# Linear layer after attention: operand splits packed into three steps, conversion steps moved between block products

## Chip, cores and metric

The kernel runs on one core of a Trainium2 chip. The metric is the device time of one execution in microseconds. Five engines work side by side, each through its own list of instructions in order: PE (TensorE, matrix products), DVE (VectorE), ACT (ScalarE), POOL (GpSimd) and SP (SyncE, which here only issues DMAs).

## What is computed

The reference, cut to what matters. Attention with head mixing gives x, and a two-layer network with silu follows:

```python
scores = einsum('bhij,hg->bgij', scale * matmul(q, k^T), w_pre)
attn = einsum('bhij,hg->bgij', softmax(scores), w_post)
x = matmul(attn, v) as (1792, 768)
h = x @ w_in            # (768, 2048)
g = h * sigmoid(h)
return g @ w_out        # (2048, 768)
```

The two weight matrices come as 64-bit floats; all else is 32-bit.

## The kernel before, in words

**Attention** runs first, in groups, until about 440 us of the profiled execution. The change does not touch it.

**The first linear layer** is a 2x2 block product done with seven block products instead of eight. The code counts them as m = 0 to 6. Each block product has its own weight block (a sum of quarter blocks of `w_in`) and its own activations (`xs`, sums and differences of the attention output). It is done in two runs, u = 0 and 1 (the two halves of the tokens), of HF = 8 steps each. A step is one output tile of 128x448: nine matmuls at line 645, for HC = 3 chunks of the contraction. Each chunk takes three, since both operands are split into a high and a low part: high weights by high activations, high by low, and low by high, in this order. So PE needs the low activations from the fourth matmul of a step on and the low weights from the seventh on. There are 7 x 2 x 8 = 112 steps; step s belongs to block product s // 16. The first two steps are done inside attention. "Block 5" below means the block product m = 5, which is steps 80 to 95.

What one step puts on the queues stands in the last loop of the function (lines 886 to 931), in this order: the product; `ready_part` (split of a piece of weights: ACT copies the high part at line 615, POOL subtracts at 616); `load_part` (a DMA on SP, line 610); `evacuate` of the step before (out of one of seven PSUM banks, by ACT or DVE, with silu on ACT at 816); a delayed sum (836); then the jobs of the list `active`, one stage of each; then the conversion steps.

**Operand splits.** `halve` (line 647) makes the high activations by a copy on ACT (650) and, one step later, the low ones by a subtraction on DVE (652). Run (m, u) reads `ops[u]`, which the run before last used, so its three splits are put on the eight steps of the run right ahead of it, by `put_at` at line 672. `put_at(s, n, todo)` spreads the jobs evenly over n steps. `subtract` (654 to 656) forms the differences of activations on DVE, also by `put_at`.

**Weight pieces.** Each block's weights come in six pieces of four chunks, first to sixth. They are loaded and split over the second run of the block before and the first steps of their own block.

**Conversion.** `convert` (lines 38 to 100) is a generator that turns the 64-bit weights into the 32-bit sums that the block products read. It does 96 conversions, two to a piece of the result: the first half of them, for `w_in`, is done in attention, the rest, for `w_out`, later. A conversion is three steps of the generator, with four instructions on DVE (lines 86, 63, 92, 93), one on ACT (90), one multiplication on POOL (66) and, at every second conversion, four additions on POOL (69 to 72); SP loads its source (47) and stores a finished sum (57). In attention some 60 of the 96 are begun. In the linear layer the table `PACE` says how many steps of the generator a block product takes, spread evenly over its 16 steps. At the first step of the second run of block 6 whatever is left is done at once.

Nothing reorders any of this: the order in the code is the order on each engine.

Of the kernel before, what the change touches and what calls it, by code (L numbers as in the profile page):

```python
# [103 lines left out]
def talking_heads_then_silu_mlp(  # L104
# [46 lines left out]
    HF, HC = NFC // 2, NCC // 2  # L151
# [323 lines left out]
    for n in range(1, len(seq)):  # L475
        p0, p1 = first[n - 1], first[n]
        spread = (0, 0, 0, 0, 2, 2) if n == 1 else (-6, -5, -4, -2, -1, 0) if p1 - p0 == 12 else (-6, -5, -4, -3, -2, -1)
        for h in range(0 if n > 1 else 2 * NE, H, 2):
            i = p0 + spread[h // 2]
# [99 lines left out]
    step_of = {x: s for s, x in enumerate(steps)}  # L579
# [67 lines left out]
    def halve(src, dst):  # L647

        hi, lo = (dst[:, 0], dst[:, 1]) if not isinstance(dst, tuple) else dst
        nc.scalar.copy(out=hi, in_=src)  # L650
        yield
        nc.vector.tensor_sub(out=lo, in0=src, in1=raw(hi))  # L652
# [9 lines left out]
    def put_at(s, n, todo):  # L662

        for m, what in enumerate(todo):
            begin[s + m * n // len(todo)].append(what)
# [3 lines left out]
    for m in range(7):  # L669
        for u in range(NU):  # L670
            if m or u:
                put_at(step_of["i", m, u, 0] - HF, HF - 1, [
                    lambda c=c, u=u, at=SOURCE[m]: halve(xs[u][(*at, c)], ops[u][c]) for c in range(HC)])
    for d, (x, y, z) in enumerate(DIFFER):
        for u in range(NU):
# [204 lines left out]
            queue.dma_start(out=out[row:row + end - n, i * W2:(i + 1) * W2], in_=t[n - c * 128:end - c * 128])  # L880
            n = end

    PACE = (18, 14, 26, 6, 18, 22, 16)
    active, sums_at = [], {}
    prev, accs = None, {}
    for s, (kind, m, u, a) in enumerate(steps):
# [41 lines left out]
        if kind == "i":  # L928
            n = u * HF + a
            for _ in range((n + 1) * PACE[m] // (NU * HF) - n * PACE[m] // (NU * HF)):  # L930
                next(conv, None)
# [27 lines left out]
```

## Time and profile before

| what | value |
| --- | --- |
| median of three runs | 856.02 us (854.14 to 858.73) |
| the profiled execution | 856.93 us, its span 855.2 us, mean clock of PE 0.982 of full speed |
| PE matmul busy | 812.8 us, 95% of the span |
| PE weight load busy | 664.4 us, 78% |
| DVE busy | 625.5 us, 73% |
| ACT busy | 509.1 us, 60% |
| POOL busy | 427.0 us, 50% |
| first linear layer | from about 440.4 to 645.1 us of the span |

Busy times of different engines overlap, so they do not add up to the span. A share over the whole span says little on a stage: the views by stretch below are to be read for that.

### The profile page before, as it was taken

How to read it: one execution, taken by the hardware profiler on the slowest of the kernel's cores; microseconds unless marked ns; L12 is line 12 of the kernel's file. 1: busy time of each engine (PE TensorE's matmuls, PEld its weight loads, DVE VectorE, ACT ScalarE, POOL GpSimd, SP SyncE). 2: the span in 40 equal slices, each digit the busy share in tenths (PEclk: the TensorE clock that was granted, in tenths of full speed). 3: DMA queues.
4: the chain of work that ended last, by engine and by line, in shares of the span. 5: the costliest groups of instructions: out<-in, count | busy, mean ns of one | idle time of the engine just before them, and what ended most of it. 6: DMA issues, size and time to landing. Idle time of an engine off the chain costs nothing.

```text
span 855.2 us, 27554 instructions
## 1 busy us (share of the span) xinstructions
PE 812.8 (95%) x11148; PEld 664.4 (78%) x11148; DVE 625.5 (73%) x1137; ACT 509.1 (60%) x1114; POOL 427.0 (50%) x693
## 2 busy tenths in 40 slices
PE   7989999899989999799899999999999999999997
PEld 5456665566756666566589999998989999999997
DVE  5554776477766777475778799999998888786343
ACT  4675887588877878587756554314576533433330
POOL 6131545444554645363787578457643444433440
PEclk9899999899999999899999999999999999999999
DMA  8668878777797787775545347335522123111133
GB/s 175 182 178 194 214 203 242 209 219 202 208 236 222 207 230 206 203 227 162 167 130 178 118 144 211 92 101 153 176 71 66 47 75 92 55 56 56 56 121 130
DMA packets 156838, 132.90 MB, mean 155 GB/s; under 512 B 52163, under 2 KB 150447, under 8 KB 156711
## 3 DMA queue, kind: packets, MB, share of 16 engines
q1 hardware_dynamic: 153459, 128.11, 52.8%
q10 hardware_dynamic: 2836, 2.37, 1.0%
q8 instruction: 88, 1.44, 0.7%
q0 software_dynamic: 416, 0.66, 0.3%
q14 instruction: 39, 0.32, 0.1%
HBM read 64.01 MB, written 27.53 MB: 107 GB/s over the span
## 4 chain that ended last, share of the span: by engine, by line
PE 71%; DVE 11%; DMA 6%; ACT 5%; issue 3%; POOL 2%; SPq 1%; ACTq 1%; DVEq 0%; POOLq 0%
PE ph L629 12%; PE ph L645 10%; PE pt L629 9%; PE pa L437 9%; PE po L368 8%; PE pt L645 7%; PE pp L399 7%; PE pqk L339 7%; DMA g<-st 4%; DVE nm L405 1%; DVE op L652 1%; ACT e L409 1%; DVE g L836 1%; ACT at L446 1%; DVE cg L92 1%
## 5 line engine op out<-in xcount | busy, mean ns | idle before, releaser
L616 POOL TENSOR_TENSOR wl<-wl,wh 128x384 fp32r<-128x384 f32 (+1 forms) x98 | 143.5, 1480 | 125.1 <-ACT wh L615 118.9
L425 POOL TENSOR_SCALAR wr<-wpost,r 128x60 f32<-128x60 f32 x184 | 72.1, 405 | 181.1 <-DVE r L422 125.0
L405 DVE TENSOR_REDUCE nm<-pp 128x1 f32<-128x448 f32 x184 | 105.9, 617 | 71.5 <-PE pp L399 70.9
L409 ACT ACTIVATE e<-pp,nm 128x448 f32<-128x448 f32 x184 | 115.4, 631 | 41.9 <-DVE nm L405 39.3
L437 PEld LDWEIGHTS pa<-wr,e 64*64 64x64 f32 (+1 forms) x5888 | 98.0, 132 | 47.1 <-issue 28.1
L437 PE MATMUL pa<-wr,e 64*64 64x60 f32 (+1 forms) x5888 | 110.4, 221 | 15.9 <-ACT at L446 7.7
L66 POOL TENSOR_TENSOR cg<-cw,cg 128x256 f32<-128x256 f32 x96 | 75.6, 787 | 72.3 <-DVE cw L63 71.4
L399 PE MATMUL pp<-g,wpre 64*64 64x448 f32 x736 | 100.8, 570 | 4.8 <-ACT e L409 4.8
L446 ACT COPY at<-pa 120x960 f32<-120x960 f32 x92 | 90.0, 978 | 5.3 <-PE pa L437 5.3
L368 PE MATMUL po<-at,v 120*64 120x120 f32 (+1 forms) x1536 | 89.6, 271 | 3.3 <-issue 3.3
L368 PEld LDWEIGHTS po<-at,v 120*64 120x64 f32 x1536 | 78.7, 141 | 15.4 <-issue 7.2
L645 PE MATMUL ph<-op,wh 128*128 128x448 f32 x384 | 88.9, 367 | 0.5 <-DVE op L652 0.5
L344 DVE COPY st<-pqk 120x448 f32<-120x448 f32 (+1 forms) x89 | 54.7, 617 | 36.4 <-PE pqk L339 22.2
L645 PEld LDWEIGHTS ph<-op,wh 128*128 128x128 f32 x384 | 71.9, 188 | 7.0 <-DVE op L652 0.9
L90 ACT ACTIVATE cg<-cg,ebias 128x256 int32<-128x256 int32 x96 | 49.6, 517 | 42.0 <-DVE cg L86 40.7
L615 ACT CAST wh<-wl 128x384 fp32r<-128x384 f32 (+1 forms) x98 | 52.0, 554 | 33.3 <-DMA wl<-wi_dram 26.2
L92 DVE SCALAR_TENSOR_TENSOR cg<-cw,cg 128x256 int32<-128x256 int32 x96 | 56.3, 586 | 18.6 <-ACT cg L90 18.3
L645 PE MATMUL pt<-op,wh 128*128 128x448 f32 x288 | 66.7, 366 | 0.6 <-ACT op L650 0.5
L645 PEld LDWEIGHTS pt<-op,wh 128*128 128x128 f32 x288 | 54.0, 188 | 5.6 <-ACT op L650 0.9
L339 PEld LDWEIGHTS pqk<-kh,qh 64*120 64x120 f32 (+1 forms) x186 | 19.0, 177 | 46.9 <-issue 17.9
L346 ACT COPY st<-pqk 120x448 f32<-120x448 f32 (+1 forms) x89 | 48.0, 539 | 6.2 <-PE pqk L339 4.6
L339 PE MATMUL pqk<-kh,qh 64*120 64x448 f32 (+1 forms) x186 | 47.2, 467 | 4.5 <-issue 2.2
(154 smaller groups left out, 1746.2 us busy)
## 6 DMA issues: line engine op xcount, KB each, us to landing
g<-st SPq DMA_DIRECT2D x132, 210.0 KB
cw<-in_moe_w_in SPq DMA_DIRECT2D x48, 256.0 KB
cw<-in_moe_w_out SPq DMA_DIRECT2D x48, 256.0 KB
wi_dram<-cg SPq DMA_DIRECT2D x24, 448.0 KB
wo_dram<-cg SPq DMA_DIRECT2D x24, 448.0 KB
wl<-wi_dram SPq DMA_DIRECT2D x42, 256.0 KB
wl<-wo_dram SPq DMA_DIRECT2D x56, 192.0 KB
g<-st SPq DMA_DIRECT2D x48, 175.0 KB
```

The costliest lines, as they stand in the source:

```text
L66: nc.gpsimd.tensor_mul(out=e, in0=m, in1=e)
L339: nc.tensor.matmul(ps[i][:m, :S], lhsT=q_[rows, hh, :m], rhs=k_[rows], start=(step == 0), stop=(step == 2))
L368: nc.tensor.matmul(po[i * D:(i + 1) * D, c * m:(c + 1) * m], lhsT=vs[b, h][:, i, j, :], rhs=ats[n][:, j, h + i, :m], start=(j == 0), stop= ...
L399: nc.tensor.matmul((self, other)[r].p[HP * c:HP * (c + 1), :S], lhsT=wpre[rows], rhs=gs[self.n][rows, o // R + c * np + p, :], start=True, ...
L405: nc.vector.tensor_reduce(out=self.nm, in_=self.p[:GP, :S], axis=AX.X, op=ALU.max, negate=True)
L409: nc.scalar.activation(out=self.e, in_=self.p[:GP, :S], func=AF.Exp, bias=self.nm, scale=1.0, accum_out=sums)
L425: nc.gpsimd.tensor_scalar(out=g.wr, in0=wpost.rearrange("p g i -> p (g i)"), scalar1=r[:, i:i + 1], scalar2=1.0, op0=ALU.mult, op1=ALU.mult)
L437: nc.tensor.matmul(half[64 * c:64 * c + m, s, j * GH:(j + 1) * GH], lhsT=g.e[rows, j * JT + c * JH:j * JT + c * JH + m], rhs=g.wr[rows], s ...
L446: nc.scalar.copy(out=ats[self.n].rearrange("p j g t -> p (j g) t")[:, :, o:o + 2 * R].rearrange("p x (c i) -> p x c i", i=RH), in_=pa[:KV] ...
L616: nc.gpsimd.tensor_sub(out=wl, in0=raw(wl), in1=raw(wh))
L629: nc.tensor.matmul(p[:, :W2], lhsT=x, rhs=w, start=(g == 0 and n == 0), stop=(g == FG - 1 and n == len(todo) - 1))
L645: nc.tensor.matmul(p[:, :T], lhsT=w, rhs=x, start=(n == 0), stop=(n == len(todo) - 1))
```

## The change

The three splits of a run are put on the first three steps of the run ahead of it, where they stood on its steps 0, 2 and 4; and ten steps of the generator are moved from blocks 5 and 6 to blocks 0 and 1. The sum of `PACE` stays 120.

```diff
     for m in range(7):
         for u in range(NU):
             if m or u:
-                put_at(step_of["i", m, u, 0] - HF, HF - 1, [
+                put_at(step_of["i", m, u, 0] - HF, HC, [
                     lambda c=c, u=u, at=SOURCE[m]: halve(xs[u][(*at, c)], ops[u][c]) for c in range(HC)])
...
-    PACE = (18, 14, 26, 6, 18, 22, 16)
+    PACE = (22, 20, 26, 6, 18, 18, 10)
```

No instruction is added or taken away on any engine, and PE's list is the same. What moves shows on the other engines. First DVE, in the steps ahead of block 5 (tiles `op00` to `op02` are the three low operands of its first run, L838 takes a product out of PSUM, L836 is a delayed sum, L86, L63, L92 and L93 are conversion). Before, ending at the third low operand:

```order
L838 TENSOR_TENSOR g111_8865<-g111_8865,ph_10163 128x448
L836 TENSOR_TENSOR g016_8854<-g016_8854,g116_8870 128x448
L86 TENSOR_SCALAR cg_10141<-cw_10055 128x256
L63 SCALAR_TENSOR_TENSOR cw_9996<-cw_9996 128x256
L838 TENSOR_TENSOR g112_8866<-g112_8866,pt_10178 128x448
L836 TENSOR_TENSOR g017_8855<-g017_8855,g117_8871 128x448
L652 TENSOR_TENSOR op01_8365<-x101_125,op01_8365 128x448
L838 TENSOR_TENSOR g113_8867<-g113_8867,pt_10199 128x448
L92 SCALAR_TENSOR_TENSOR cg_10141<-cw_10055,cg_10141 128x256
L93 TENSOR_SCALAR cw_10055<-cw_10055 128x256
L838 TENSOR_TENSOR g114_8868<-g114_8868,pt_10215 128x448
L652 TENSOR_TENSOR op02_8366<-x102_126,op02_8366 128x448
```

The same place after the change, from the first low operand to the third:

```order
L652 TENSOR_TENSOR op00_8364<-x100_124,op00_8364 128x448
L86 TENSOR_SCALAR cg_10212<-cw_10075 128x256
L63 SCALAR_TENSOR_TENSOR cw_9996<-cw_9996 128x256
L838 TENSOR_TENSOR g111_8865<-g111_8865,ph_10196 128x448
L836 TENSOR_TENSOR g016_8854<-g016_8854,g116_8870 128x448
L652 TENSOR_TENSOR op01_8365<-x101_125,op01_8365 128x448
L838 TENSOR_TENSOR g112_8866<-g112_8866,pt_10220 128x448
L836 TENSOR_TENSOR g017_8855<-g017_8855,g117_8871 128x448
L652 TENSOR_TENSOR op02_8366<-x102_126,op02_8366 128x448
```

The third subtraction (`op02`) now follows the second after one evacuation and one sum; before, two evacuations and half a conversion stood between, and two more evacuations stood ahead of it altogether. The conversion here is a later one, by about three.

Next POOL, at the pieces of weights for block 6 (each L616 is one piece; these are its first to fourth). Before:

```order
L616 TENSOR_TENSOR wl_10490<-wl_10490,wh_10533 128x512
L616 TENSOR_TENSOR wl_10517<-wl_10517,wh_10553 128x512
L66 TENSOR_TENSOR cg_10499<-cw_10388,cg_10499 128x256
L616 TENSOR_TENSOR wl_10536<-wl_10536,wh_10574 128x512
L66 TENSOR_TENSOR cg_10499<-cw_10422,cg_10499 128x256
L69 TENSOR_TENSOR cg_10499<-cg_10499 128x128
L70 TENSOR_TENSOR cg_10499<-cg_10499 128x128
L71 TENSOR_TENSOR cg_10499<-cg_10499 128x128
L72 TENSOR_TENSOR cg_10499<-cg_10499 128x128
L616 TENSOR_TENSOR wl_10577<-wl_10577,wh_10616 128x512
```

After:

```order
L616 TENSOR_TENSOR wl_10521<-wl_10521,wh_10555 128x512
L66 TENSOR_TENSOR cg_10503<-cw_10369,cg_10503 128x256
L616 TENSOR_TENSOR wl_10538<-wl_10538,wh_10576 128x512
L616 TENSOR_TENSOR wl_10558<-wl_10558,wh_10592 128x512
L66 TENSOR_TENSOR cg_10503<-cw_10420,cg_10503 128x256
L69 TENSOR_TENSOR cg_10503<-cg_10503 128x128
L70 TENSOR_TENSOR cg_10503<-cg_10503 128x128
L71 TENSOR_TENSOR cg_10503<-cg_10503 128x128
L72 TENSOR_TENSOR cg_10503<-cg_10503 128x128
L616 TENSOR_TENSOR wl_10595<-wl_10595,wh_10632 128x512
```

In both, a multiplication and four additions stand ahead of the fourth piece. Before they belong to conversion 93 (counted from 0) and two more conversions are still behind; after they belong to conversion 95, the last.

Last POOL at the pieces for block 3, again the first to the fourth. Before:

```order
L616 TENSOR_TENSOR wl_9629<-wl_9629,wh_9671 128x512
L66 TENSOR_TENSOR cg_9636<-cw_9529,cg_9636 128x256
L616 TENSOR_TENSOR wl_9654<-wl_9654,wh_9696 128x512
L616 TENSOR_TENSOR wl_9674<-wl_9674,wh_9713 128x512
L66 TENSOR_TENSOR cg_9636<-cw_9561,cg_9636 128x256
L69 TENSOR_TENSOR cg_9636<-cg_9636 128x128
L70 TENSOR_TENSOR cg_9636<-cg_9636 128x128
L71 TENSOR_TENSOR cg_9636<-cg_9636 128x128
L72 TENSOR_TENSOR cg_9636<-cg_9636 128x128
L66 TENSOR_TENSOR cg_9721<-cw_9598,cg_9721 128x256
L616 TENSOR_TENSOR wl_9716<-wl_9716,wh_9761 128x512
```

After:

```order
L616 TENSOR_TENSOR wl_9671<-wl_9671,wh_9714 128x512
L616 TENSOR_TENSOR wl_9688<-wl_9688,wh_9734 128x512
L66 TENSOR_TENSOR cg_9696<-cw_9596,cg_9696 128x256
L616 TENSOR_TENSOR wl_9717<-wl_9717,wh_9754 128x512
L66 TENSOR_TENSOR cg_9696<-cw_9616,cg_9696 128x256
L69 TENSOR_TENSOR cg_9696<-cg_9696 128x128
L70 TENSOR_TENSOR cg_9696<-cg_9696 128x128
L71 TENSOR_TENSOR cg_9696<-cg_9696 128x128
L72 TENSOR_TENSOR cg_9696<-cg_9696 128x128
L616 TENSOR_TENSOR wl_9757<-wl_9757,wh_9797 128x512
```

Before, the four additions stand one multiplication ahead of the fourth piece, and that multiplication (L66) is the last thing it stands behind; after, the last multiplication has its four additions behind it, and the fourth piece comes after them.

## Rows read from the trace of the kernel before

**Rows 1.** The head of the page: span.

```profile
span 855.2 us, 27554 instructions
```

**Rows 2.** Windows by block product 0 to 6; each engine: busy us (x instructions), granted clock.

```profile
440.40:466.04 25.64, 25.64 (x128) 23.78 (x127) 21.62 (x40) 15.91 (x35) 16.91 (x21) 1.00 0.46 144
466.04:495.23 29.19, 29.19 (x146) 27.05 (x144) 24.18 (x41) 16.86 (x31) 17.25 (x22) 1.00 0.44 139
495.23:524.41 29.18, 29.18 (x145) 27.05 (x144) 28.17 (x45) 17.18 (x36) 24.08 (x29) 1.00 0.56 175
524.41:553.59 29.18, 29.18 (x145) 27.05 (x144) 27.11 (x43) 9.47 (x19) 18.35 (x19) 1.00 0.35 102
553.59:582.79 29.20, 29.20 (x145) 26.97 (x144) 28.92 (x50) 8.18 (x16) 17.36 (x18) 1.00 0.51 154
582.79:613.61 30.82, 29.92 (x146) 26.88 (x144) 28.92 (x55) 15.69 (x31) 21.50 (x29) 1.00 0.48 149
613.61:645.08 31.47, 29.98 (x146) 26.81 (x144) 30.06 (x51) 23.41 (x46) 16.26 (x19) 1.00 0.29 88
```

**Rows 3.** Timeline of PE: start us, us, instruction [idle before <-releaser].

```profile
582.79 1.18 PE L645 MATMUL ph<-op,wh 128*128 128x448 f32 x5
584.47 0.47 PE L645 MATMUL ph<-op,wh 128*128 128x448 f32 x1 [0.50 <-DVE op L652]
...
589.39 0.47 PE L645 MATMUL pt<-op,wl 128*128 128x448 f32 x1 [0.40 <-POOL wl L616]
...
623.17 0.88 PE L645 MATMUL ph<-op,wl 128*128 128x448 f32 x3 [0.89 <-POOL wl L616]
...
630.41 1.46 PE L645 MATMUL pt<-op,wh 128*128 128x448 f32 x4 [0.47 <-ACT op L650]
...
645.08 0.69 PE L629 MATMUL ph<-wh,op 128*128 128x384 f32 x3
```

**Rows 4.** Groups by line on DVE, 440.4 to 645.08: xcount | busy us, mean ns | idle before.

```profile
L92 DVE SCALAR_TENSOR_TENSOR cg<-cw,cg 128x256 int32<-128x256 int32 x36 | 27.3, 757 | 3.5 <-ACT cg L90 3.5
L63 DVE SCALAR_TENSOR_TENSOR cw<-cw 128x256 f32<-128x256 uint32 x37 | 20.6, 556 | 0.0
...
L86 DVE TENSOR_SCALAR cg<-cw 128x256 int32<-128x256 int32 x36 | 19.2, 534 | 0.0
L93 DVE TENSOR_SCALAR cw<-cw 128x256 int32<-128x256 int32 x36 | 17.8, 493 | 2.4
```

**Rows 5.** Tile cg, 440.4 to 645.08: duration ns min/median/max.

```profile
L92 DVE SCALAR_TENSOR_TENSOR cg<-cw,cg x36: 407/680/1518, 445.7 to 627.4; 128x256 int32<-128x256 int32 x36
```

**Rows 6.** Timeline of DVE before the wait at 584.47.

```profile
581.97 0.98 DVE L92 SCALAR_TENSOR_TENSOR cg<-cw,cg 128x256 int32<-128x256 int32 x1
...
583.80 0.62 DVE L652 TENSOR_TENSOR op<-x,op 128x448 fp32r<-128x448 f32 x1
```

**Rows 7.** Timeline of POOL before the waits at 589.39 and 623.17.

```profile
585.04 0.75 POOL L66 TENSOR_TENSOR cg<-cw,cg 128x256 f32<-128x256 f32 x1 [2.37 <-DVE cw L63]
...
618.72 0.75 POOL L66 TENSOR_TENSOR cg<-cw,cg 128x256 f32<-128x256 f32 x1 [1.29 <-DVE cw L63]
...
621.47 2.95 POOL L616 TENSOR_TENSOR wl<-wl,wh 128x512 fp32r<-128x512 f32 x2
```

**Rows 8.** Timeline of ACT before the wait at 630.41.

```profile
628.79 1.11 ACT L816 ACTIVATE g<-g 128x448 f32<-128x448 f32 x2 [0.61 <-DVE g L846]
```

**Rows 9.** Timelines of DVE, POOL and PE around the start of block product 3.

```profile
528.07 0.68 DVE L63 SCALAR_TENSOR_TENSOR cw<-cw 128x256 f32<-128x256 uint32 x1
...
526.66 0.87 POOL L66 TENSOR_TENSOR cg<-cw,cg 128x256 f32<-128x256 f32 x1 [0.36 <-DVE cw L63]
...
529.84 0.74 POOL L66 TENSOR_TENSOR cg<-cw,cg 128x256 f32<-128x256 f32 x1
530.54 3.31 POOL L616 TENSOR_TENSOR wl<-wl,wh 128x512 fp32r<-128x512 f32 x2
...
532.92 0.77 PE L645 MATMUL ph<-op,wl 128*128 128x448 f32 x3
```

## Prediction, made before the changed kernel was run

> **What bounds the kernel now.** The profiled execution took 856.93 us; its span is 855.2 [rows 1], so 1.73 us lie around it. PE is busy nearly throughout, so the first thing to ask is where PE is not busy in the stage that the change touches. I cut the first linear layer at the first step of each block product and read the busy times by window [rows 2]. In blocks 0 to 4 PE is busy all the time, and a block of 16 steps takes 29.18 to 29.20 us, 1.824 us a step. Block 5 takes 30.82 and block 6 takes 31.47. The granted clock is 1.00 in all seven windows, the upper level of 2.4 GHz, so the clock is not the reason. The two last blocks together are 62.29 us long, by the start of block 5 and the start of the second layer [rows 3], against 2 x 29.19 = 58.38 at full pace. **So 3.9 us of PE time are lost in this stage, all of it in blocks 5 and 6.** That is all that this change can give back: 0.46% of the time, just under the 0.5% that a measurement of this kernel can tell from no change.
>
> PE's timeline names four waits [rows 3], and the idle time shown for each is only a part of its price, since a late operand also breaks up the overlap of weight loads. Each goes back to DVE. At 584.47 PE waits for the third low operand of block 5; DVE, in order, was still at a conversion when it was due [rows 6]. At 589.39 it waits for a piece of low weights on POOL, which stood behind a conversion multiplication that had itself waited 2.37 us for DVE's line 63 [rows 7]. At 623.17 it is the same: the multiplication at 618.72 waited 1.29 us for DVE, four additions followed, and the piece began only at 621.47 [rows 7]. At 630.41 it waits for a high operand on ACT, which stood behind an activation that waited for a DVE evacuation [rows 8]. DVE is what is late: it is busy 28.9 of 29.2 us in block 4, 28.9 of 30.8 in block 5, 30.1 of 31.5 in block 6; but 21.6 of 25.6 in block 0 and 24.2 of 29.2 in block 1 [rows 2].
>
> **The change part by part.** *Moved conversion.* Ten generator steps are 3.33 conversions. On DVE one conversion is four instructions with means of 757, 556, 534 and 493 ns [rows 4], 2.34 us together, so 7.8 us of DVE work move. Block 0 takes 4 of the steps, 3.1 us, where DVE has 25.64 - 21.62 = 4.0 us free; block 1 takes 6, 4.7 us, where it has 29.19 - 24.18 = 5.0 free. It just fits, and PE does not see it, since operands and weights of blocks 1 and 2 are made several steps early. What if that cover is too short? The same instruction of line 92 took between 407 and 1518 ns [rows 5], 0.54 to 2.0 times its mean; a whole conversion scaled so costs 1.26 to 4.7 us, and the moved work 4.2 to 15.6 us. Against 9.0 free, the upper end overflows by 6.6. I take the mean, since it is over 36 conversions of this very stage.
>
> The spread of one instruction at one shape shows that something off DVE holds it up. The Trainium skill ("SBUF — State Buffer", Who interferes with whom) says that a DVE instruction with two SBUF inputs contends with a GpSimd instruction that reads SBUF, and that the loser fully blocks. By that rule the conversions put beside the subtractions and POOL additions of block 0 would be paid near the upper end; no row here separates the two causes.
>
> Blocks 5 and 6 lose the same 7.8 us on DVE. In block 6 the generator is then exhausted before its first evacuations, so its POOL, ACT and SP queues hold weight work alone from there. The two late waits, at 623.17 and 630.41, should go. The 4 steps (3.1 us) taken out of block 5 are over twice the 1.29 us by which DVE held up the multiplication at 618.72. The moved DMAs (47 and 57 on SP) pass loads of weights in blocks 0 to 2, but each waits only for POOL work that stands ahead of the same pieces on POOL anyway, so I cost them at nothing beyond what POOL is costed at below; if a store held a load back longer, a piece would be late by that much.
>
> *Splits in the first three steps.* Nothing is added. The third low operand of a run moves ahead of an evacuation, half a conversion (lines 92 and 93) and another evacuation. The half conversion alone is 0.76 + 0.49 = 1.25 us [rows 4], while the operand was late by 0.5 us [rows 3]. So the wait at 584.47 goes. The evacuations and conversions that now come behind it are later by up to two subtractions, and next due there are PSUM banks, of which there are seven, 12.8 us of PE work: covered. In block 6 the third high operand is copied two steps (3.6 us) earlier in ACT's order, which also speaks for the wait at 630.41 going. The wait at 589.39 hangs on a conversion multiplication ahead of a piece. After the change other multiplications stand ahead of the pieces of block 5, so this one is moved rather than removed.
>
> *New waits.* Where conversion 81 takes the place of 78, block 3 is the tight spot. Before, the piece that PE needed at 532.92 was made from 530.54 on, two pieces in 3.31 us, so it was ready at 532.2, 0.7 us in time [rows 9]. Afterwards it stands behind a multiplication and four additions. That multiplication waits for the line 63 that takes the place of the one at 528.07 to 528.75 [rows 9]. Ahead of it in block 2 stands one line 92 and one line 93 less, 1.25 us; so without any delay carried over from blocks 0 and 1 it ends at 527.5. A multiplication with its additions took from 526.66 to 529.84, 3.18 us [rows 9]; then 1.66 for the piece: ready at 532.3, 0.6 in time. Delay carried into block 2 I put between 0 and 1.5 us (the 1.2 us that would be left free in blocks 0 and 1, and as much the other way): 0.1 late at the middle, 0.9 at the worst. I take **0.2**. In block 5 a piece stands behind a multiplication and its additions again, as the one at 623.17 did; that wait was 0.89 [rows 3], so its bounds are 0 and 0.9, and I take **0.5**.
>
> *Sum:* 856.93 - 3.9 + 0.2 + 0.5 = 853.7 us for the profiled execution. It lay 0.9 us above the median of the runs shown, so on the scale of that median the forecast is 856.02 - 3.2 = **852.8 us**.
>
> **The rivals.** *A. Forecast:* nearly all of the 3.9 us comes back, 852.8.
>
> *B. The waits move.* DVE's total work is unchanged, and it has 0.3 to 2 us free in each of blocks 2 to 5 [rows 2]. If the delay at the start of block 2 is 1.5 us and block 5 pays its 0.9, perhaps twice over, about 0.9 + 1.2 = 2.1 of the 3.9 are paid back: 854.2. For it: block 3 has hardly any margin. Against: block 3 itself leaves DVE 2.1 us free, so a delay does not reach block 4.
>
> *C. It does not do what it says.* Idle time of DVE in blocks 0 and 1 could be time in which it waits for a product to evacuate, not spare time; moved work then pushes evacuations later, all of blocks 2 to 5 runs late as now, and as much is lost as is won: 856. Against: evacuations have seven banks of room.
>
> *D. Slower.* The moved conversions are paid at the top price, 15.6 us. Of the 6.6 us that do not fit, block 2 absorbs its free 1.0; the fourth piece of block 3 is then ready at 532.3 + 5.6 = 537.9, and PE waits 5.0 us there. That alone is 5.0 - 3.9 = +1.1, 857.1; if DVE stays late, the waits at 584.47 and 589.39 remain too (30.82 - 29.19 = 1.6 us of the 3.9): 858.7. It decides once a moved conversion costs more than (9.0 + 1.0 + 0.6 + 3.9) / 3.33 = 4.4 us. Against: the mean is 2.34.
>
> **How the numbers follow.** A 0.62, B 0.2, C 0.1, D 0.08. Two lone medians of this kernel can differ by more than a microsecond (its runs span 854.14 to 858.73), so A alone spans 850.9 to 854.6. From its lower end, where all of the 3.9 is kept (852.1) and the median falls 1.2 lower, the range goes up through B and C to D's first figure: 850.9 to 857.1. Faster by over 0.5% means under 851.74, more than this stage has to give, so only the scatter or a gain outside the stage makes it: a quarter of A, 0.16. Slower by over 0.5% means over 860.3, the far end of D with scatter: 0.05. The rest, 0.79, is within 0.5%.
>
> **What would show it.** Blocks 5 and 6 at 29.2 to 29.8 us each by the starts of their first steps; no PE wait for ACT's line 650 or DVE's line 652; no conversion instruction on any engine in the second half of block 6; DVE in blocks 0 and 1 busy all but 1 or 2 us, in block 6 with some 4 us free. Wrong would be: a wait of PE for POOL's line 616 in steps 48 to 56, above 1 us; blocks 0 to 3 longer than 29.2; a mean of the four conversion lines above 3 us in blocks 0 and 1; or blocks 5 and 6 still over 30.5.

## The result, and the profile after

The change made the kernel slower: 864.16 us (median of 11 runs, 859.79 to 866.35) against 857.54 us for the kernel before in the same comparison. The ratio is 1.0069, with a 95% interval of 1.0043 to 1.0096. (A ratio, here and below, leaves out executions more than 1.5% above the fastest of the same kernel and is not simply the quotient of two medians.) The forecast was 852.8 us in a range of 850.9 to 857.1, so the time lies outside the range and on the other side of the kernel before.

The profiled execution of the changed kernel took 861.12 us, 4.19 more than that of before. I read it in the order of the prediction: first the layer by block products. These are the windows by block, with the columns of [rows 2].

```profile
440.79:466.44 25.65, 25.65 (x129) 23.77 (x127) 23.22 (x41) 13.51 (x31) 17.52 (x21) 1.00 0.45 143
466.44:496.33 29.89, 29.43 (x145) 26.96 (x144) 27.90 (x50) 19.29 (x37) 21.49 (x29) 1.00 0.58 172
496.33:527.77 31.44, 29.45 (x145) 26.96 (x144) 26.79 (x45) 16.26 (x36) 23.69 (x30) 1.00 0.52 160
527.77:559.59 31.82, 29.85 (x145) 26.89 (x144) 30.48 (x47) 11.33 (x24) 17.99 (x19) 1.00 0.42 126
559.59:588.77 29.18, 29.18 (x145) 27.04 (x144) 28.87 (x49) 7.27 (x14) 17.65 (x21) 1.00 0.42 132
588.77:620.11 31.34, 29.84 (x145) 26.81 (x144) 29.79 (x54) 17.17 (x34) 22.92 (x27) 1.00 0.44 135
620.11:649.30 29.19, 29.19 (x146) 27.04 (x144) 22.88 (x39) 22.51 (x43) 11.09 (x12) 1.00 0.21 62
```

Set each block against 29.19 us. Block 6 has got back all it had lost. Block 5 still loses 2.15. Blocks 1, 2 and 3, clean before, now lose 0.70, 2.25 and 2.63. The layer takes 208.5 us (440.79 to 649.30) against 204.7 (440.40 to 645.08): **3.8 of the 4.2 us lie in this stage**, and the granted clock is 1.00 in every window. The other 0.4 us lies outside the layer. I use the layer's own loss as the measure below: the layer starts anywhere between 436 and 446 us in these traces, although the change does not touch attention, which scatters the whole time by some us, while the loss at a wait repeats to about 0.1 us where the same work lies ahead of it.

PE's timeline names five waits in the layer.

```profile
472.33 0.47 PE L645 MATMUL pt<-op,wl 128*128 128x448 f32 x1 [0.46 <-POOL wl L616]
...
509.02 0.67 PE L645 MATMUL ph<-op,wl 128*128 128x448 f32 x2 [1.99 <-POOL wl L616]
...
529.56 0.88 PE L645 MATMUL pt<-op,wl 128*128 128x448 f32 x3 [0.41 <-POOL wl L616]
...
538.81 0.88 PE L645 MATMUL ph<-op,wl 128*128 128x448 f32 x3 [1.55 <-POOL wl L616]
...
599.21 0.87 PE L645 MATMUL ph<-op,wl 128*128 128x448 f32 x3 [1.50 <-POOL wl L616]
```

The waits for operands on DVE and ACT [rows 3] are gone. All five are for a piece of low weights on POOL: the third piece of block 1, the fifth of block 2, the first and fourth of block 3, the fourth of block 5. By the starts of the steps they cost 0.7, 2.3, 0.7, 1.8 and 1.8 us; 0.6 us more lies in steps without a named wait.

Why is the piece late? POOL's timeline ahead of the dearest wait:

```profile
503.74 1.19 POOL L66 TENSOR_TENSOR cg<-cw,cg 128x256 f32<-128x256 f32 x1 [1.83 <-DVE cw L63]
504.88 0.46 POOL L69 TENSOR_TENSOR cg<-cg 128x128 f32<-128x128 f32 x1
...
506.44 0.92 POOL L72 TENSOR_TENSOR cg<-cg 128x128 f32<-128x128 f32 x1
507.32 2.94 POOL L616 TENSOR_TENSOR wl<-wl,wh 128x512 fp32r<-128x512 f32 x2
```

It is the pattern of [rows 7]: a multiplication waits for DVE's line 63 (here 1.83 us), four additions follow, and only then comes the piece. The same stands ahead of the other four pieces, where the multiplication waited 0.77, 2.37, 0.56 and 1.30 us for line 63. POOL is late because DVE is. DVE's own timeline shows how late, at the start of block 2:

```profile
495.18 0.61 DVE L830 TENSOR_TENSOR g<-ph,g 128x448 f32<-128x448 f32 x1
495.71 1.34 DVE L86 TENSOR_SCALAR cg<-cw 128x256 int32<-128x256 int32 x1
496.97 1.51 DVE L63 SCALAR_TENSOR_TENSOR cw<-cw 128x256 f32<-128x256 uint32 x1
498.40 0.61 DVE L830 TENSOR_TENSOR g<-ph,g 128x448 f32<-128x448 f32 x1
500.06 0.56 DVE L92 SCALAR_TENSOR_TENSOR cg<-cw,cg 128x256 int32<-128x256 int32 x1 [1.05 <-ACT cg L90]
500.73 1.33 DVE L93 TENSOR_SCALAR cw<-cw 128x256 int32<-128x256 int32 x1
501.98 0.61 DVE L830 TENSOR_TENSOR g<-ph,g 128x448 f32<-128x448 f32 x1
```

The evacuation of block 1's last product starts at 501.98, 5.6 us after block 2 began (496.33). In the kernel before it started at 495.60, 0.4 us after block 2 began there (495.23):

```profile
495.60 0.60 DVE L830 TENSOR_TENSOR g<-ph,g 128x448 f32<-128x448 f32 x1
```

A reader should also see the bracket in the fence before that: 1.05 us in which DVE, already late, waits for ACT. A late engine that still idles is what the prediction left out.

How much of it? Take one window in each trace, from step 2 of the layer to that evacuation. Busy DVE is the third pair; first before, then after.

```profile
440.40:495.60 55.20, 55.20 (x274) 51.19 (x273) 46.18 (x81) 32.77 (x66) 34.54 (x41) 1.00 0.45 142
```

```profile
440.79:501.98 61.19, 60.73 (x300) 55.98 (x299) 55.62 (x95) 35.05 (x72) 44.31 (x53) 1.00 0.53 162
```

DVE's idle time in it was 9.0 us and is now 5.6. **The added work is 9.4 us (55.62 - 46.18); only some 3.4 of it went into idle time, and 6.0 came out as delay (61.19 - 55.20).** What is left idle is named by DVE's waits in the same two windows, before and after:

```profile
DVE g L830 <- PE ph L645: 2.8, 3, 1.2
DVE cg L92 <- ACT cg L90: 2.0, 2, 1.7
DVE op L652 <- POOL wl L616: 1.6, 1, 1.6
DVE g L830 <- PE pt L645: 1.1, 2, 0.5
DVE op L652 <- ACT op L650: 0.6, 1, 0.6
```

```profile
DVE cg L92 <- ACT cg L90: 2.8, 6, 1.0
DVE op L652 <- POOL wl L616: 1.7, 1, 1.7
```

The waits for PE (3.9 us) were capacity, and the change used them up. The wait for POOL at the very start and those for ACT at line 92 were not: they stay, and those for ACT grow. (The waits named after the change are 4.5 of the 5.6 us; the rest has no name in the view.)

### The profile page after: what moved, and what is told of

Its sections match the earlier page's. It is cut to its first block, busy times and chain, and to the rows that moved or that the text cites. A ratio compares the mean times of both kernels' runs of the same rounds, so it can differ in the third digit from the quotient of the medians.

```text
span 859.4 us, 27558 instructions
## 1 busy us (share of the span) xinstructions
PE 810.6 (94%) x11148; PEld 662.0 (77%) x11148; DVE 626.2 (73%) x1137; ACT 509.9 (59%) x1114; POOL 427.5 (50%) x693
## 3 DMA queue, kind: packets, MB, share of 16 engines
q10 hardware_dynamic: 2836, 2.37, 1.0%
## 4 chain that ended last, share of the span: by engine, by line
PE 66%; DVE 11%; DMA 7%; POOL 5%; ACT 4%; issue 3%; SPq 2%; ACTq 0%; POOLq 0%; DVEq 0%
PE ph L629 12%; PE pt L629 9%; PE pa L437 9%; PE po L368 7%; PE ph L645 7%; PE pp L399 7%; PE pqk L339 7%; PE pt L645 6%; DMA g<-st 5%; DVE op L652 2%; DVE g L836 1%; DVE nm L405 1%; POOL cg L66 1%; POOL wl L616 1%; DVE cg L92 1%
## 5 line engine op out<-in xcount | busy, mean ns | idle before, releaser
L616 POOL TENSOR_TENSOR wl<-wl,wh 128x384 fp32r<-128x384 f32 (+1 forms) x98 | 142.4, 1471 | 134.5 <-ACT wh L615 130.7
L66 POOL TENSOR_TENSOR cg<-cw,cg 128x256 f32<-128x256 f32 x96 | 76.8, 800 | 66.6 <-DVE cw L63 65.7
L368 PE MATMUL po<-at,v 120*64 120x120 f32 (+1 forms) x1536 | 87.4, 268 | 1.0 <-DMA v<-in_v 1.0
L92 DVE SCALAR_TENSOR_TENSOR cg<-cw,cg 128x256 int32<-128x256 int32 x96 | 55.0, 573 | 19.3 <-ACT cg L90 19.0
L645 PE MATMUL ph<-op,wl 128*128 128x448 f32 x192 | 50.0, 368 | 5.0 <-POOL wl L616 5.0
```

Of the source, the lines that this page charges most:

```text
L66: nc.gpsimd.tensor_mul(out=e, in0=m, in1=e)
L368: nc.tensor.matmul(po[i * D:(i + 1) * D, c * m:(c + 1) * m], lhsT=vs[b, h][:, i, j, :], rhs=ats[n][:, j, h + i, :m], start=(j == 0), stop= ...
L616: nc.gpsimd.tensor_sub(out=wl, in0=raw(wl), in1=raw(wh))
L645: nc.tensor.matmul(p[:, :T], lhsT=w, rhs=x, start=(n == 0), stop=(n == len(todo) - 1))
```

## The experiments

The theories. *Table*: the ten moved steps alone cause the loss, not the splits. *Load*: more work was put into blocks 0 and 1 than DVE can hold, it enters block 2 late, and whatever stands ahead of a piece is late with it. *Order*: the loss comes from which multiplication now stands ahead of which piece. *Queue*: the moved stores (line 57) and loads on SP hold up the loads of weights. Loss is the layer's in the trace, by the starts of its steps (before 4.0, after 7.9); the ratio is against the kernel before in the same job.

**The splits alone**: the table of before.

```diff
-    PACE = (22, 20, 26, 6, 18, 18, 10)
+    PACE = (18, 14, 26, 6, 18, 22, 16)
```

> The splits on the first three steps alone, with the old table of conversion steps. In the changed kernel blocks 1, 2, 3 and 5 lose 0.7, 2.2, 2.6 and 2.2 us of PE time, all of it in waits for low weights on POOL. Table theory (the ten moved conversion steps make those waits): here blocks 0 to 3 lose under 0.3 us each; blocks 5 and 6 lose 1 to 3 us, less than the 3.9 of before, since the wait for the third low operand and that for the third high operand are gone; ratio 0.997 to 1.000. Splits theory (packing the splits holds conversion back in the first steps of a run, and the weights behind it): blocks 1 to 3 lose 3 us or more here too, ratio 1.003 to 1.007.

Measured 858.72 us, ratio 1.0007 (0.9977 to 1.0036). The layer loses 2.9: 0.9 in block 5 and 1.9 in block 6, nothing in blocks 1 to 4. The splits give back about 1.1 us in the layer, too little for the total to tell, and alone cause none of the new waits.

**The table alone**: the splits where they were.

```diff
-                put_at(step_of["i", m, u, 0] - HF, HC, [
+                put_at(step_of["i", m, u, 0] - HF, HF - 1, [
```

> The new table of conversion steps alone, with the old splits. Table theory: blocks 1 to 3 lose 4 to 7 us as in the changed kernel, block 6 loses nothing, block 5 loses 1 to 3; ratio 1.003 to 1.008. Splits theory: blocks 1 to 3 lose under 1 us, ratio 0.995 to 1.000.

Measured 861.49 us, ratio 1.0047 (1.0014 to 1.0079). It loses 6.6: 1.0, 4.2, 0.7 and 0.6 in blocks 1, 2, 3 and 5, none in block 6. The table theory stands: the new waits come with the table, with or without the splits. Block 5 lost less than it expected, and the two parts do not simply add: beside the new table, the packed splits take 1.9 us off block 2 but put 1.9 on block 3 and 1.5 on block 5, so there they cost 1.2 us in the layer (7.9 against 6.6) where with the old table they gave back 1.1.

**Stores later**: each moved store (line 57) is issued three generator steps later, behind loads that it stood ahead of.

```diff
-        else:
+        elif k < 60:
             store()
...
-        yield
+        yield store() if k % 2 and k >= 60 else None
```

> The changed kernel, with each finished sum of the linear layer's conversion stored three generator steps later, so that on SP fewer loads of weights stand behind a store that waits for POOL's additions. Only SP's order changes. Queue theory (the new waits come from weight loads held back on SP): the first load of block 3, issued at 522.3 us in the changed kernel, 5.4 us after its place, goes out by 519, DVE's idle time in blocks 2 and 3 behind ACT falls from 4.7 to under 2 us, and blocks 2 and 3 together lose under 2.5 us where they lost 4.9; ratio against the kernel before 0.999 to 1.004. Load theory (DVE is simply late): the loads go out earlier, yet the pieces on POOL still stand behind multiplications that wait for DVE, and blocks 2 and 3 lose 4 to 6 us as now; ratio 1.004 to 1.009.

Measured 860.44 us, ratio 1.0043 (1.0006 to 1.0079). The first load of block 3 is issued 2.7 us earlier (78.8 us after the start of step 2 of the layer, 81.5 in the changed kernel), yet the loss is 7.2 and blocks 1 to 3 are as before: 0.7, 2.3, 2.8. In its trace the piece of block 2 still stands behind a multiplication that waits for DVE in the same way. The queue theory falls for blocks 1 to 3; only block 5's loss fell, from 2.2 to 1.4.

**A lighter conversion in the same order**: line 93 is left out from conversion 60 on, so the second weight matrix is not the reference's, and one of DVE's four instructions goes while all the rest stays where it is.

```diff
-        nc.vector.tensor_scalar(out=hi, in0=hi, scalar1=0xFFFFF, scalar2=1 << WEXP, op0=ALU.bitwise_and, op1=ALU.bitwise_or)
+        if k < 60: nc.vector.tensor_scalar(out=hi, in0=hi, scalar1=0xFFFFF, scalar2=1 << WEXP, op0=ALU.bitwise_and, op1=ALU.bitwise_or)
```

> The changed kernel without line 93 (the masking of the mantissa) for the conversions from number 60 on, so that the second weight matrix comes out with wrong values: 0.5 us of DVE work less at each of 36 conversions, 18 us in the layer, all queues otherwise the same. Load theory: with DVE no longer late, blocks 1 to 3 lose under 1.5 us together where they lost 5.6, and block 5 under 0.5; ratio 0.994 to 0.998. Order theory (the waits come from the four additions that now stand ahead of a piece, however early DVE is): the waits at the fifth piece of block 2 and the fourth piece of block 3 stay above 1 us each; ratio 1.000 to 1.005.

Measured 855.23 us, ratio 0.9964 (0.9935 to 0.9994). PE waits for nothing in the layer. These are its windows for blocks 0 to 3:

```profile
438.77:464.42 25.65, 25.65 (x129) 23.77 (x128) 23.51 (x37) 15.12 (x34) 18.58 (x21) 1.00 0.50 158
464.42:493.61 29.19, 29.19 (x146) 27.05 (x145) 26.74 (x42) 18.65 (x37) 23.85 (x30) 1.00 0.57 177
493.61:522.80 29.19, 29.19 (x146) 27.05 (x145) 25.36 (x37) 17.97 (x38) 23.71 (x30) 1.00 0.60 185
522.80:552.00 29.20, 29.20 (x146) 27.06 (x145) 25.91 (x42) 9.35 (x19) 17.44 (x17) 1.00 0.36 110
```

With the order of the changed kernel on every engine and a lighter DVE, all waits are gone. The order alone is not the cause: without so much work on DVE it costs nothing. (DVE still waits for ACT at line 92 for 6.0 us in blocks 0 to 3, but PE waits for nothing by it.) It lightens the last blocks as well, so it says nothing on how much may be moved.

**Six steps moved instead of ten**, all with the splits:

```diff
-    PACE = (22, 20, 26, 6, 18, 18, 10)
+    PACE = (20, 18, 26, 6, 18, 18, 14)
```

> The changed kernel with six steps moved into blocks 0 and 1 (2 and 4) instead of ten: two whole conversions, so that in blocks 2 to 4 every piece of weights stands behind the same kind of conversion instruction, with or without the four additions, as before the change. Load theory (about half of DVE's free time in blocks 0 and 1 cannot be used, some 4.6 of the 9.0 us can): 2 x 2.2 = 4.4 us just fit, and blocks 1 to 3 lose under 1.5 us together where ten steps lost 5.6; blocks 5 and 6 lose 0 to 2. Order theory (what stands directly ahead of a tight piece decides): blocks 1 to 3 lose under 0.3 as well, so this run tells the two apart only together with the next.

Measured 855.40 us, ratio 0.9983 (0.9946 to 1.0020). The layer loses 1.1, of it 1.0 at one step of block 5; blocks 1 to 4 and 6 are clean. The window from step 2 to the evacuation of block 1's last product, as above:

```profile
435.99:491.01 55.02, 55.02 (x273) 51.00 (x272) 51.13 (x88) 33.42 (x69) 38.70 (x46) 1.00 0.50 155
```

DVE does 5.0 us more than before (51.13 against 46.18) and is on time: the evacuation starts at 491.01, 0.2 us after block 2 began. Its idle time fell from 9.0 to 3.9, and of these 3.0 are named in its waits:

```profile
DVE op L652 <- POOL wl L616: 1.7, 1, 1.7
DVE cg L92 <- ACT cg L90: 0.8, 2, 0.5
DVE g L830 <- PE ph L645: 0.5, 1, 0.5
```

So the two blocks took in about 5 of the 9 us, not 9; the wait for POOL is as long as before, while the waits for ACT are shorter than before (2.0) and longer with ten steps (2.8).

**Twelve steps**: `PACE = (23, 21, 26, 6, 18, 18, 8)`.

> The changed kernel with twelve steps moved into blocks 0 and 1 (5 and 7): four whole conversions, so the same kind of instruction stands ahead of each piece of blocks 2 to 4 as before, as with six, but DVE has 1.4 us more to do there than in the changed kernel. Load theory: blocks 1 to 3 lose 5 to 9 us, no less than the 5.6 of the changed kernel; ratio 1.004 to 1.010. Order theory: under 1.5 us as with six moved; ratio 0.997 to 1.001.

Measured 860.51 us, ratio 1.0045 (1.0013 to 1.0077), loss 6.5: 2.3, 0.0 and 2.5 in blocks 1 to 3 and 1.6 in block 5. Blocks 1 to 3 lose 4.8, just under what the load theory expected. So the loss does not simply grow with the load: ten steps cost 5.6 there. Block 1 loses more and block 2 nothing, so **the load makes DVE late, and the order decides which piece meets the delay**. In block 0, which takes 2, 4 and 5 of them, DVE is busy 23.2 us with six, with ten and with twelve steps moved.

**Line 90 one generator step earlier**, to take away DVE's waits for ACT:

```diff
-        if before:
-            finish(*before)
+        if before: finish(*before)
+        if k >= 60: nc.scalar.activation(out=e, in_=e, func=AF.Relu, scale=8.0, bias=ebias)
         yield True
-        nc.scalar.activation(out=e, in_=e, func=AF.Relu, scale=8.0, bias=ebias)
+        if k < 60: nc.scalar.activation(out=e, in_=e, func=AF.Relu, scale=8.0, bias=ebias)
```

> The changed kernel with the conversion's activation (line 90) put on ACT one generator step earlier, right behind the DVE instruction that it waits for, from conversion 60 on; only ACT's order changes, so that DVE's line 92 less often waits for an activation that stands behind a weight cast that waits for its DMA. Mutual wait theory (part of DVE's lateness is idle time spent waiting for ACT: 5.9 us at line 92 in blocks 0 to 3 of the changed kernel): that idle falls under 3 us and blocks 1 to 3 lose 2 to 4 us where they lost 5.6. Plain load theory (DVE's work alone is too much): the idle only turns up elsewhere, ACT waits longer for DVE and the weight casts are later, blocks 1 to 3 lose 5 to 8.

Measured 858.81 us, ratio 1.0016 (0.9979 to 1.0053), loss 5.9. DVE's waits for ACT at line 92 in blocks 0 to 3, the changed kernel first, then this one (where the moved activation stands at line 88):

```profile
DVE cg L92 <- ACT cg L90: 5.9, 9, 1.6
```

```profile
DVE cg L92 <- ACT cg L88: 0.7, 3, 0.2
```

Block 2's loss falls from 2.3 to 0.4; blocks 1 and 3 stay at 0.7 and 2.6. So of 5.6 us in blocks 1 to 3, 1.9 hang on the waiting of DVE for ACT, and 3.7 remain without it. This fits the run with twelve steps, where block 2 was clean: there DVE waited 2.5 us at line 92 up to 530 us, against 5.9 in the changed kernel.

**Five steps out of block 6 alone, two into block 0 and three into block 3** (against the kernel before): `PACE = (20, 14, 26, 9, 18, 22, 11)`.

> A candidate: the splits on the first three steps, and five steps of conversion taken out of block 6 alone, two to block 0 and three to block 3, where DVE is not late (table 20, 14, 26, 9, 18, 22, 11). With the splits alone block 5 lost 0.9 us and block 6 1.9. Load theory: blocks 0 to 4 lose under 0.3 us, block 6 nothing, block 5 up to 1.5; total loss 0 to 1.7 against 4.0 before, ratio 0.995 to 0.999. If the piece order decides instead, a loss of over 1 us shows in blocks 2 to 4.

Measured 859.24 us, ratio 1.0024 (0.9990 to 1.0057), loss 3.9: 0.6 in block 3, 1.4 in block 5, 1.8 in block 6. The expectation missed: blocks 3 and 6 and the total lie above its ranges, and the sign of the order theory, over 1 us in blocks 2 to 4, did not show either. All four waits that PE's view names are for pieces on POOL. It gains nothing to speak of in the layer (4.0 before).

**Six steps and line 90 earlier**, the two that helped together:

> Six steps moved, and the conversion's activation one generator step earlier on ACT. With six moved and nothing else 1.1 us were lost, 1.0 of it at the third piece of block 5. If the mutual wait of DVE and ACT is in that piece's way too, the loss falls under 0.5 us; if not, it stays at 0.7 to 1.5. Blocks 0 to 3 lose nothing by either. Ratio 0.994 to 0.999.

Measured 854.08 us, ratio 0.9943 (0.9912 to 0.9974): faster than the kernel before and, by the ratios, than the changed one. The layer loses 0.9, 0.8 of it at the third piece of block 5, as with six steps alone (1.0). POOL's timeline there:

```profile
582.12 0.76 POOL L66 TENSOR_TENSOR cg<-cw,cg 128x256 f32<-128x256 f32 x1 [1.82 <-DVE cw L63]
...
584.45 0.73 POOL L72 TENSOR_TENSOR cg<-cg 128x128 f32<-128x128 f32 x1
585.14 1.28 POOL L616 TENSOR_TENSOR wl<-wl,wh 128x512 fp32r<-128x512 f32 x1
```

DVE is late again ahead of this multiplication, by the same 1.8 us with line 90 early or not. What makes it late there was not tried.

**Six steps once more**, the kernel of *Six steps moved instead of ten*, for a sharper time:

> The kernel with six steps moved once more, for a narrower interval and to see whether its losses repeat: 0.9 to 1.3 us in the whole layer, at the third piece of block 5 again. 4.0 - 1.1 = 2.9 us of 858 is a ratio of 0.9966; by it, a ratio of 0.994 to 0.999.

Measured 854.86 us over six runs, ratio 0.9896 (0.9845 to 0.9948), below what was expected. The ratio rests on four of the six runs, one of which, at 844.72, lies 7 us below the next; the medians over all runs, 854.86 and 859.07, stand as 0.995 to 1, inside the expected range. So I do not take it for a larger gain than the 3.0 us (0.3%) of the first trace, which is argued, not shown.

The losses did not repeat as expected: the layer of its trace loses 2.3 us, not 0.9 to 1.3. The wait at the third piece of block 5 is there again and costs 1.1 us, blocks 1 to 4 are clean again, but from that wait to the end of the layer every step takes 1.860 us where it took 1.824, with no wait named and a granted clock of 1.00: 1.0 us over 27 steps. Such steps follow waits in other traces too, for four steps in the kernel before (84 to 87) and three in the changed one (49 to 51). Why they last, here to the end, is open.

## Why the prediction was wrong

- **The step that failed is "It just fits" in *Moved conversion*.** It set 7.8 us of work against 9.0 us of free time. The work measured 9.4 us over the same stretch, and the four conversion lines are busy by as much more (below): by their counts 3.5 conversions more, not 3.33, and 2.7 us for each, since the others became a little longer too. The larger error is the 9.0: idle time was read as capacity, and only some 3.4 us of it took in work (5.1 with six steps). The time in which DVE waits for POOL is there in all three windows, before and with six and ten steps (1.6 to 1.7 us), and the time in which it waits for ACT at line 92 came back, longer, with ten.
- **The delay carried into block 2** was put at 0 to 1.5 us and measured 5.6 (0.4 before the change). The terms behind it failed with it. The two tight places were named rightly, the fourth piece of block 3 and a piece of block 5, again the fourth, and put at 0.2 and 0.5 us; they cost 1.8 each. The waits at the third piece of block 1, the fifth of block 2 and the first of block 3, 3.7 us together, were not foreseen.
- That **"operands and weights of blocks 1 and 2 are made several steps early"** does not hold for the low weights while conversions stand among them on POOL: PE waited for a piece in both blocks.
- **Right:** the waits for lines 650 and 652 went. Block 6 is back at 29.19 us, with no conversion on DVE after 621.6, and DVE there has 6.3 us free. The mechanism by which a conversion multiplication hands DVE's lateness to a piece was right too, and so was B's remark that block 3 keeps a delay from block 4, which loses nothing. Of its signs of being wrong there came a wait of over 1 us in steps 48 to 56 (1.55), blocks 1 to 3 longer than 29.2 us and, of blocks 5 and 6, block 5 over 30.5; a conversion above 3 us did not.
- **The SP loads costed at nothing** did come later, but that is not what PE waits for in blocks 1 to 3 (stores later: a load 2.7 us earlier, the same loss). In block 5 it may be worth 0.8.
- **The rivals.** C was nearest in its outcome: idle time in blocks 0 and 1 that is not spare, and what follows late. But it named the wrong idle time: the waits for a product (3.9 us) are the part that was filled, and those for POOL and ACT are the part that was not. It let the layer lose as much as before, 3.9 us, where it lost 7.9. It was argued away with the seven PSUM banks; but the delay does not reach PE through evacuations, it reaches PE through POOL. D had the right sign by the wrong price: its top price was 4.7 us a conversion, and in the stretch of blocks 0 and 1 a conversion cost 2.29 us by the means of its lines, against 2.18 before. As to the rule of the Trainium skill ("SBUF — State Buffer", Who interferes with whom), by which the loser of a contention is fully blocked: the packed blocks show a rise of 5% in these means, far from the upper end. Yet the spread does go with POOL, which the prediction left open: in the layer of the trace before, line 92 took 407 to 424 ns in the 9 places where POOL ran nothing beside it and up to 1518 ns beside line 616, while line 838, which reads one operand from PSUM, took 606 to 615 ns either way (spans on POOL are rough). So the mean of a conversion already holds this price, before the change as after it; of the conversion instructions in the stretch, 26 of 42 ran with nothing on POOL beside them before, 27 of 56 after. In the timeline of the changed kernel shown above, lines 86 and 63 took 1.34 and 1.51 us from 495.71 on, beside this:

```profile
495.61 4.02 POOL L616 TENSOR_TENSOR wl<-wl,wh 128x512 fp32r<-128x512 f32 x3
```

The groups of the four conversion lines on DVE in that stretch, with the columns of [rows 4], before and then after:

```profile
L92 DVE SCALAR_TENSOR_TENSOR cg<-cw,cg 128x256 int32<-128x256 int32 x10 | 7.0, 703 | 2.0 <-ACT cg L90 2.0
L86 DVE TENSOR_SCALAR cg<-cw 128x256 int32<-128x256 int32 x11 | 5.6, 509 | 0.0
L93 DVE TENSOR_SCALAR cw<-cw 128x256 int32<-128x256 int32 x10 | 5.3, 527 | 0.6
...
L63 DVE SCALAR_TENSOR_TENSOR cw<-cw 128x256 f32<-128x256 uint32 x11 | 4.8, 440 | 0.0
```

```profile
L92 DVE SCALAR_TENSOR_TENSOR cg<-cw,cg 128x256 int32<-128x256 int32 x14 | 9.3, 662 | 2.8 <-ACT cg L90 2.8
L93 DVE TENSOR_SCALAR cw<-cw 128x256 int32<-128x256 int32 x14 | 7.8, 560 | 0.9
L86 DVE TENSOR_SCALAR cg<-cw 128x256 int32<-128x256 int32 x14 | 7.5, 533 | 0.0
L63 DVE SCALAR_TENSOR_TENSOR cw<-cw 128x256 f32<-128x256 uint32 x14 | 7.5, 533 | 0.0
```

The sum, mended: of 4.0 us lost before, 2.3 in block 6 are recovered and block 5 loses 0.5 more than its 1.6; with 5.6 new in blocks 1 to 3 that is 4.0 - 2.3 + 0.5 + 5.6 = 7.8, against 7.9 measured. What stays open: what delays DVE at the start of block 5, and why the total's ratio (0.69%) stands above the layer's 3.8 us (0.45%), though its interval reaches down to 0.43%.

## What to carry to other kernels

Do not read all idle time of an in-order engine as capacity. Here the waits for the bound engine were filled first; the wait for POOL stayed, and those for ACT shrank or grew with what was added. Take off the waits for other engines that may still be there, and test the rest by how late the engine is at the end of the stage. A delay shows where a shared queue (here POOL's) puts late work ahead of something that the bound engine needs, not where the late engine's own buffers lie. Move a smaller part first: here six of the ten steps won back 3.0 of the 4.0 us in one trace and 1.8 in another, and all ten turned the gain into a loss.

## What the runs showed that I had not expected

- DVE was busy 23.21, 23.22 and 23.23 us of block 0's 25.65 with six, ten and twelve steps moved: what was added above six did not raise it. It is no hard limit, since without line 93 it was 23.51.
- A late DVE does not stop waiting: at line 92 it waited for ACT 5.9 us in blocks 0 to 3 of the changed kernel, 2.2 before, though it was later. Issuing line 90 one generator step earlier brought that to 0.7.
- The whole time of one program scatters by some us while single waits inside it repeat closely: the wait in block 1 costs 0.72 or 0.71 us and that in block 2 2.26 or 2.27 in two traces whose layers start 5.5 us apart (the changed kernel and *Stores later*). The steps after a wait need not repeat, as *Six steps once more* shows.
